# A recurrent attention kernel with a mixture of experts: a shorter lead-in, routing steps at other places of the order, and output scatters without an order among themselves

## The chip, the core and the metric

The kernel runs on one core of one Trainium2 chip. The metric is the device time of one execution in microseconds. Three runs of the kernel before gave 429.65, 430.54 and 431.69 us (median 430.54); the execution that the profiler recorded took 428.78 us, and its span from the first to the last instruction is 426.8 us. All times "at 133 us" below count from the start of that span.

Engines by the names of the profile: PE is the matrix engine (PEld its weight loads), DVE the vector engine, ACT the scalar engine, POOL the GpSimd engine and SP the sync engine, which here only issues DMAs. "SPq", "ACTq" and "POOLq" are the instruction queues of these engines.

## The reference

```python
# attention: B, H, S, D = 4, 8, 768, 48; everything is float32
for t in range(S):
    cur = einsum('bhd,bhe->bhde', u * k[t], v[t])
    y[t] = einsum('bhd,bhde->bhe', r[t], state + cur)
    state = w * state + einsum('bhd,bhe->bhde', k[t], v[t])
# bridge: x = y as N = 3072 rows of 384
# router and experts: E = 8, F = 1024
logits = normalised(x) @ normalised(expert_emb).T / tau
e = argmax(logits);  gate = softmax(logits)[e]
out[row] = gate[row] * (relu(x[row] @ w1[e]) @ w2[e])
```

Each row goes to one expert, and each expert's rows are computed together.

## The kernel before

**Attention.** The sequence is cut into 6 chunks of 128 steps; with 4 batches this makes 24 units (`i = 4 * chunk + batch`), and `attention` (L800 on) runs them one after the other, with the steps of several units interleaved in an order written out by hand (`tc.manual_schedule()`: the program order is the order on every engine). Within a unit, `turn_r` and `turn_k` transpose r and the scaled k on PE; the first is multiplied on DVE to `RT` (L328), the second copied by ACT to `KT` (L339). `scores` (L349) multiplies the two, `masked` (L355) writes the masked scores `AT` on DVE, and `sums` (L401, L410) multiplies them with V on PE, after which ACT copies the result to `yT` (L415). `rows` turns it back and adds, on DVE (L434), `xd`, the product of V with `diag`. That `diag` is reduced on DVE (`own_sum`, L303) from `KU`, two POOL products (`own`, L296 and L297) that need the tile `u_bc`, which ACT's queue loads (L123). In the order of DVE the reduction `diag` of a unit stands before the two `AT` of the same unit. Unit rows X go to a DRAM buffer `xs` (`put`, L618, SP's queue).

**Lead-in.** `build_first` (L46) loads the decay, makes its powers, turns them (`kpT`, L91) and scales the first k. It issues ten products of constants whose result is not used (`wake`, L67): six ahead of `kpT`, four behind it. `build_consts` then issues the other loads on ACT's queue, the constants on POOL, and copies on ACT.

**Router.** For each chunk (group) the steps `logits`, `choose`, `before`, `ranks`, `places`, `exps`, `gates`, `located`, `listed` and `taken` follow, spread over later units. `exps` (L601 to L604) is three small DVE operations and one exponential on ACT. `listed` calls `slices`, which makes two one-hot matrices on DVE (`lane` L637, `sel` L643) and from `sel` two POOL products (`what`, L647 and L648); `taken` (L663) multiplies `what` with `lane` on PE.

**Early experts.** After four of the six chunks `settle` (L699 to L721, ten DVE operations) names the two experts with the fewest rows so far (`LAST`), and SP loads their weights (w1 and w2, 1.5 MB each, both experts at once). One tile of rows of each is gathered (L931, POOL) and computed by `Early` while the router of the last chunks finishes; `fill(n)` puts n of its steps between steps of the router.

**Experts.** `experts` then works through eight blocks. Block i has up to four tiles of rows, gathered with indirect DMAs (L1001). Products use a seven-product scheme on halves: `weigh` and `weigh_out` combine the weights (`Sw`, `Tw`), `halves` combines the hidden rows (`Sh`), `hidden` and `out` do the products, `plain` does block 0's first layer in the usual way. Results are written to the output with indirect DMAs of POOL (`put`, L1259; `Early` at L966), each of which names the whole output tensor as its destination. [...]The last block ends with `out`, which puts two tiles.

Of the kernel before, what the change touches and what calls it, by code (L numbers as in the profile page):

```python
# [19 lines left out]
N = B * S  # L20
# [16 lines left out]
W_MIN, W_MAX = 0.7, 1.4  # L37
TS = 32
TG = TT // TM
WAKE = (6, 4)  # L40
AHEAD = 5


# [4 lines left out]
def build_first(k):  # L48


    nc, pool = k.nc, k.aconst
    wc = pool.tile([128, NP], F32, name="wc")
    nc.vector.memset(wc, 1.0)
    with nc.allow_non_contiguous_dma(reason="384 words"):
        for s, q in ((0, nc.sync), (1, nc.scalar)):
            q.dma_start(out=wc[s * DP : s * DP + D, :], in_=k.w.rearrange("(p s) d -> s d p", s=2)[s])
    k.ones = k.const.tile([128, 128], F32, name="ones")
    nc.vector.memset(k.ones, 1.0)
    wide = k.work.tile([128, 512], F32, name="wide", tag="AT1")
    nc.vector.memset(wide, 1.0)  # L60
    k.ident = k.const.tile([128, 128], F32, name="ident")
    make_identity(nc, k.ident)

    def wake(count):
        ps = k.ps.tile([128, 512], F32, name="wake", tag="y")
        for _ in range(count):
            nc.tensor.matmul(ps, k.ones, wide, start=True, stop=True)  # L67

    wake(WAKE[0])
    for lst, name, count in ((k.Kpad, "Kpad", 4), (k.Rpad, "Rpad", AHEAD + 2)):  # L70
        for i in range(count):
            t = pool.tile([128, H, DP], F32, name=f"{name}{i}")
            nc.gpsimd.memset(t[:, :, D:DP], 0.0)
            lst.append(t)
    load(k, 0, nc.scalar)


    nc.vector.tensor_scalar(wc, wc, W_MIN, W_MAX, ALU.max, ALU.min)
    t = pool.tile([128, NP, C], F32, name="wpow")
    for p in range(NP):  # L80
        nc.vector.tensor_tensor_scan(
            t[:, p, :], wc[:, p : p + 1].to_broadcast([128, C]), k.ones, 1.0, ALU.mult, ALU.mult
        )
    mid = pool.tile([128, NP], F32, name="mid")
    nc.vector.reciprocal(mid, t[:, :, C // 2])
    over_i = mid[:, :, None].to_broadcast([128, NP, C])
    kp = k.work.tile([128, NP, C], F32, name="kp", tag="AT0")
    nc.vector.tensor_mul(kp, t[:, :, ::-1], over_i)
    ps = k.ps.tile([128, NP, 2, DP], F32, name="kpT", tag="xp")
    for p in range(NP):  # L90
        nc.tensor.transpose(ps[:, p].rearrange("q s d -> q (s d)"), kp[:, p, :], k.ident)  # L91
    wake(WAKE[1])
    k.rpow = pool.tile([128, NP, C], F32, name="rpow")
    nc.vector.tensor_mul(k.rpow, t, over_i)
    cols = ps[:, :, :, 0:D]
    nc.vector.tensor_mul(
        k.Kpad[0].rearrange("q (p s) d -> q p s d", s=2)[:, :, :, 0:D],
        k.loaded[0][0].rearrange("q (p s) d -> q p s d", s=2), cols,
    )
    k.kpow = pool.tile([128, H, D], F32, name="kpow")  # L100
    nc.vector.tensor_copy(k.kpow.rearrange("q (p s) d -> q p s d", s=2), cols)  # L101
    k.wC = t[:, :, C - 1 : C].to_broadcast([128, NP, D])


# [8 lines left out]
def build_consts(k):  # L113
# [19 lines left out]
    k.wrow = k.aconst.tile([1, DM], F32, name="wrow")  # L133
    nc.scalar.dma_start(out=k.wrow, in_=k.w.rearrange("(o h) d -> o (h d)", o=1))
    k.yT = [k.aconst.tile([128, 2, NP // 2, C], F32, name=f"yT{i}") for i in range(2)]
    for t in k.yT:
        nc.gpsimd.memset(t, 0.0)
    for b in range(B):
        t = k.aconst.tile([128, NP, D], F32, name=f"state{b}")
        nc.gpsimd.memset(t, 0.0)  # L140
# [487 lines left out]
    return tile_, place  # L628


def slices(k, c, slots, tile_, place):


    nc, p = k.nc, k.rt
    n = slots.shape[1]
    lane = p.tile([128, B, 128], F32, name="lane", tag="lane", bufs=1)
    nc.vector.tensor_tensor(  # L637
        lane, k.lanes[:, None, :].to_broadcast([128, B, 128]),
        place[:, :, None].to_broadcast([128, B, 128]), ALU.is_equal,
    )  # L640
    sel = p.tile([128, B, n], F32, name="sel", tag="sel")
    full = [128, B, n]
    nc.vector.tensor_tensor(  # L643
        sel, slots[:, None, :].to_broadcast(full), tile_[:, :, None].to_broadcast(full), ALU.is_equal
    )
    what = p.tile([128, B, 2, n], F32, name="what", tag="what")
    nc.gpsimd.tensor_mul(what[:, :, 0, :], sel, k.token[:, c, :, None].to_broadcast(full))  # L647
    nc.gpsimd.tensor_mul(what[:, :, 1, :], sel, k.gate[:, c, :, None].to_broadcast(full))  # L648
    return lane, what


def located(k, g):
    g.spots = spots(k, g.c)


def listed(k, g):
    g.lane, g.what = slices(k, g.c, k.slots.rearrange("p e t -> p (e t)"), *g.spots)


def taken(k, g, tag="st"):  # L660
# [134 lines left out]
def attention(k):  # L795
# [17 lines left out]
    for i in range(-1, units):  # L813
        j = i - SETTLED * B
        if 0 < i + AHEAD < units:
            load(k, i + AHEAD)
        if i < 2:
            next(emb)
        whole(summed, i - 6)
        whole(places, i - 4)  # L820
        whole(logits_out, i - 3)
        on(turn_r, i + 1)
        if i < units - 1:
            on(own_rows, i, 0)
        on(turn_k, i + 1)
        whole(turn_logits, i - 3)
        on(scaled, i + 2)
        for n in (0, 1) if i < 0 else (i + 2,):
            on(own, n)
        on(states, i)  # L830
        of_group(squares, i - 1)
        if i < units - 1:
            on(own_rows, i, 1)
        whole(norms, i - 2)
        whole(choose, i - 3)
        whole(before, i - 3)
        whole(exps, i - 4)
        whole(located, i - 4)
        whole(gates, i - 5)
        whole(listed, i - 5)  # L840
        on(own_sum, i + 1)
        if i == units - 2:
            own_rows_once(k, i + 1)
        if j == 10:
            k.lists = turned_lists(k, perm, "st")
            lists = taken_by_rank(k, k.lists)
            first = [Early(k, r, *lists, w) for r, w in zip(LAST, k.weights)]
        on(sums, i)
        on(carry, i)
        on(scores, i + 1)  # L850
        on(masked, i + 1, 0)
        on(rows, i)
        on(masked, i + 1, 1)
        of_group(put, i)
        of_group(turn_rows, i - 1)
        whole(logits, i - 2)
        whole(ranks, i - 3)
        whole(taken, i - 5)
        if i == B:
            decays(k)  # L860
        if i == 2:
            build_turned(k)
        if 3 <= i < 3 + len(k.ring):
            k.nc.gpsimd.memset(k.ring[i - 3], 0.0)
        if j == 7:
            load_, count = loads(k, "st")
        if j == 8:
            settle(k, load_, count)
            for w, r in zip(k.weights, LAST):
                load_weights(k, expert_number(k, r), w)  # L870
        if j == 9:
            perm = turner(k, k.by)
        if j == 10:
            to = outs(k, lists[0], E * TM)

# [4 lines left out]
    def fill(count):  # L880
        for _ in range(count):
            next(early, None)

    gates(k, g)
    first[0].turn()
    turn_rows(k, h, B - 1)
    listed(k, g)
    squares(k, h, B - 1)
    norms(k, h)
    logits(k, h)  # L890
    first[1].turn()
    logits_out(k, h)
    fill(1)
    turn_logits(k, h)
# [6 lines left out]
    places(k, h)  # L901
    exps(k, h)
    located(k, h)
    summed(k, g)
    by = order(k, load_, k.settled)
    perm = turner(k, by)
    gates(k, h)
    listed(k, h)
    fill(4)
    taken(k, h, "tp")  # L910
    summed(k, h)
    fill(1)
# [9 lines left out]
class Early:  # L922
# [23 lines left out]
    def steps(self, to):  # L946
# [14 lines left out]
        for f in range(NF):  # L961
            nc.tensor.matmul(ps, self.hT[:, f, :], self.weights[1][:, f, :], start=(f == 0), stop=(f == NF - 1))
            if f == NF - 1:
                y = k.work.tile([128, DM], F32, name="earlyy", tag="xd")
                nc.scalar.mul(y, ps, self.gate)
                nc.gpsimd.indirect_dma_start(  # L966
                    out=k.out[:, :], out_offset=IndirectOffsetOnAxis(ap=to[:, self.col], axis=0), in_=y[:, :],
                    in_offset=None, bounds_check=N - 1, oob_is_err=False,
                )
            yield  # L970


# [23 lines left out]
def gather(k, take, to, gate, n=128):  # L996
# [6 lines left out]
        bounds_check=N - 1, oob_is_err=False,  # L1003
    )
    return G, to, gate, n


def gathers(k, r):
# [52 lines left out]
class Block:  # L1061
# [194 lines left out]

    def put(self, t, y):
        k, (_, j, _, here) = self.k, self.tiles[t]
        k.nc.gpsimd.indirect_dma_start(  # L1259
            out=k.out[:, :], out_offset=IndirectOffsetOnAxis(ap=k.to[0:here, j : j + 1], axis=0), in_=y[0:here, :],  # L1260
            in_offset=None, bounds_check=N - 1, oob_is_err=False,
        )


def combined(eng, t1, t2, t3, t4, b11, b12, b21, b22):
# [20 lines left out]
def experts(k):  # L1286
# [20 lines left out]
        b.turn()  # L1307
    do(blocks[1].Tx)
    do(blocks[1].weigh())
    blocks[0].plain()  # L1310
    first_weights(2)
    blocks[2].gather()
    do(blocks[0].halves())
    for i in range(E):
        doubled = blocks[i].weigh_out()
        for b in at(i + 1):
            b.hidden(doubled)
        do(doubled)
# [15 lines left out]
def all_lists(k):  # L1334

    nc = k.nc
    with ExitStack() as ctx:
# [1 line left out]
        slots = numbers(k, "allslots", [128, SLOTS], [[1, SLOTS]], 0, 0)  # L1339
        sums = k.ps.tile([128, 2, SLOTS], F32, name="allsums", tag="y")  # L1340
        for c in range(NCH):
            lane, what = slices(k, c, slots, *spots(k, c))
            for b in range(B):
                i = c * B + b
                nc.tensor.matmul(
# [91 lines left out]
def kernel(  # L1437
# [30 lines left out]
    n.x_dram = tc.dram_tile([128, S, D // 4], F32, name="x_dram")  # L1468
    n.need_dram = tc.dram_tile([E, TG], I32, name="need_dram")

    n.Rpad, n.Kpad, n.state = [], [], []
    for name in ("loaded", "KU", "diag", "xd", "RT", "KT", "at", "AT", "st", "y", "groups"):
        setattr(n, name, {})
    n.weights = [weight_tiles(n) for _ in range(2)]
# [43 lines left out]
```

## Time and profile before

| stretch, us | what runs | PE busy, us |
|---|---|---|
| 0 to 14 | lead-in | 14.0 (the unused products included) |
| 14 to 132 | units 0 to 21 | 116.5 of 118 |
| 132 to 144 | units 22, 23 | 10.2 of 12 |
| 144 to 160 | router of the last chunks, early experts begin | 11.5 of 16 |
| 160 to 178 | early experts | 17.3 of 18 |
| 178 to 412 | eight blocks | 232.4 of 234 |
| 412 to 427 | the last two scatters, end of the program | 0.3 of 15 |

The table is read from the busy time of each engine in each stretch. "Busy" counts an engine that is executing; where PE's figure falls short of the stretch, PE stood waiting. DVE is busy 251.1 us of the span, ACT 171.5, POOL 161.8.

### The profile page before, as it was taken

Reading aid. Unit: us, or ns where it says so; the run is one execution under the profiler, and the core shown is the slowest. Engines: PE = TensorE matmul, PEld = TensorE weight load, DVE = VectorE, ACT = ScalarE, POOL = GpSimd, SP = SyncE. Lnnn points to the kernel's source line nnn. Section 1 sums busy time; section 2 is a strip of 40 time slices with the busy share of each in tenths; the row PEclk is TensorE's granted clock in tenths of the full one; section 3 lists DMA queues with packets and bytes.
Section 4 is the critical chain, followed back from the end, with each engine's and each line's share of the span. In section 5 each row is a group of like instructions: output and inputs, shape, how many; then the busy total and the mean of one; then the engine's idle time right before and its main releaser. Section 6 shows DMA issues by size and latency. Waiting matters only on the chain. (4 is left out here: it accounts for less than half of the span.)

```text
span 426.8 us, 9300 instructions
## 1 busy us (share of the span) xinstructions
PE 399.8 (94%) x3556; PEld 355.6 (83%) x3556; DVE 251.1 (59%) x608; ACT 171.5 (40%) x517; POOL 161.8 (38%) x219
## 2 busy tenths in 40 slices
PE   8899999999999689999999999999999999999960
PEld 4688888888887578689999999999999999799660
DVE  4677786867688553137775767066376366566110
ACT  3487676767776301323323233223323323232110
POOL 7978777767673314210140241130330330300210
PEclk9999999999999999999999999999999999999995
DMA  9987676777715932133734424235255240320110
GB/s 165 189 181 154 137 150 127 149 151 150 151 39 183 389 133 88 35 75 131 251 126 149 166 77 154 81 138 185 58 179 172 62 172 28 112 92 17 39 42 21
DMA packets 93800, 54.39 MB, mean 127 GB/s; under 512 B 76937, under 2 KB 88380, under 8 KB 93746
## 3 DMA queue, kind: packets, MB, share of 16 engines
q1 hardware_dynamic: 89024, 43.85, 39.2%
q0 software_dynamic: 3296, 9.44, 6.8%
q8 instruction: 30, 0.49, 0.5%
q10 hardware_dynamic: 1426, 0.41, 0.4%
q14 instruction: 24, 0.20, 0.2%
HBM read 44.45 MB, written 9.63 MB: 127 GB/s over the span
## 5 line engine op out<-in xcount | busy, mean ns | idle before, releaser
L1259 POOL DMA_INDIRECT out_dram<-y,to x25 | 30.5, 1222 | 179.7 <-issue 91.5
L1135 PE MATMUL ps<-xTe,w 128*128 128x192 f32 (+3 forms) x336 | 63.0, 327 | 0.0
L1135 PEld LDWEIGHTS ps<-xTe,w 128*128 128x128 f32 x336 | 55.8, 190 | 0.5
L312 ACT ACTIVATE xd<-V,diag 128x48 f32<-128x48 f32 x184 | 46.3, 326 | 0.4 <-DVE diag L303 0.4
L355 DVE TENSOR_TENSOR AT<-at,umask 128x512 f32<-128x512 f32 x48 | 32.9, 686 | 23.1 <-PE at L349 23.1
L1142 ACT ACTIVATE hT<-hT 128x384 f32<-128x384 f32 (+3 forms) x42 | 22.0, 523 | 33.8 <-DVE hT L1165 21.1
L1199 PE MATMUL ps<-Tw,Sh 128*128 128x192 f32 x192 | 32.5, 326 | 0.0
L1199 PEld LDWEIGHTS ps<-Tw,Sh 128*128 128x128 f32 x192 | 31.4, 190 | 0.0
L349 PE MATMUL at<-RT,KT 48*128 48x128 f32 x384 | 27.9, 284 | 2.7 <-ACT yT L415 1.5
L1001 POOL DMA_INDIRECT G<-xs,take x25 | 26.3, 1053 | 9.8 <-PE ps L1135 2.7
L1135 PE MATMUL ps<-Tx,Sw 128*128 128x192 f32 (+3 forms) x168 | 29.7, 326 | 0.0
L349 PEld LDWEIGHTS at<-RT,KT 48*128 48x128 f32 x384 | 23.4, 187 | 7.3 <-issue 2.3
L1135 PEld LDWEIGHTS ps<-Tx,Sw 128*128 128x128 f32 x168 | 27.6, 190 | 0.1
L1152 DVE TENSOR_TENSOR u<-ps,p 128x384 f32<-128x384 f32 (+3 forms) x14 | 7.8, 557 | 31.7 <-PE ps L1135 30.9
L410 PE MATMUL y<-AT,V 128*48 128x128 f32 (+1 forms) x384 | 26.2, 277 | 0.0
L516 ACT COPY xT<-xp 128x384 f32<-128x384 f32 x24 | 11.5, 479 | 34.7 <-PE xp L514 34.7
L297 POOL TENSOR_TENSOR KU<-KU,Rpad 128x384 f32<-128x384 f32 x24 | 24.1, 1003 | 1.9
L296 POOL TENSOR_TENSOR KU<-K,u_bc 128x384 f32<-128x384 f32 x24 | 24.1, 1003 | 0.0
L288 POOL TENSOR_TENSOR Kpad<-K,kpow 128x384 f32<-128x384 f32 x23 | 23.0, 1000 | 1.7 <-DVE kpow L101 1.7
L1199 PE MATMUL ps<-w,hT 128*128 128x192 f32 x128 | 23.4, 326 | 0.0
L410 PEld LDWEIGHTS y<-AT,V 128*48 128x48 f32 (+1 forms) x384 | 20.2, 124 | 3.4 <-issue 3.4
L1199 PEld LDWEIGHTS ps<-w,hT 128*128 128x128 f32 x128 | 21.3, 190 | 0.3
(240 smaller groups left out, 810.7 us busy)
## 6 DMA issues: line engine op xcount, KB each, us to landing
w<-in_moe_w_dram SPq DMA_DIRECT2D x16, 1536.0 KB, 7.0
K<-in_k_dram SPq DMA_DIRECT2D x24, 192.0 KB, 3.2
V<-in_v_dram SPq DMA_DIRECT2D x24, 192.0 KB, 4.1
xs<-X SPq DMA_DIRECT2D x24, 192.0 KB, 2.0
Rpad<-in_r_dram SPq DMA_DIRECT2D x23, 192.0 KB, 4.0
G<-xs,take POOLq DMA_INDIRECT x27, 3.1
out_dram<-y,to POOLq DMA_INDIRECT x25, 3.1
Rpad<-in_r_dram ACTq DMA_DIRECT2D x1, 192.0 KB, 4.2
```

The costliest lines, as they stand in the source:

```text
L288: k.nc.gpsimd.tensor_mul(k.Kpad[i % len(k.Kpad)][:, :, 0:D], k.loaded[i][0], k.kpow)
L296: nc.gpsimd.tensor_mul(KU, K, k.u_bc)
L297: nc.gpsimd.tensor_mul(KU, KU, R[:, :, 0:D])
L312: k.nc.scalar.mul(k.xd[i][:, h, :], V[:, h, :], diag[:, h : h + 1])
L349: nc.tensor.matmul(at[s][:, p, :], KT[rows, p, :], RT[rows, p, :], start=True, stop=True)
L355: k.nc.vector.tensor_mul(a, k.at[i][s], k.umask[:, None, :].to_broadcast([128, NP, C]))
L410: mm(y[s][u * DP : u * DP + n, q, :], V[:, h * D : h * D + n], AT[s][:, p, :], start=(c == 0 and q == 0), stop=True, skip_group_check=True,)
L1001: nc.gpsimd.indirect_dma_start(out=G[0:n, :], out_offset=None, in_=k.xs[:, :], in_offset=IndirectOffsetOnAxis(ap=take[0:n], axis=0), bound ...
L1135: nc.tensor.matmul(ps[:, j, :], weights[:, (f + j) * 128 : (f + j + 1) * 128], moving, start=(first and j == 0), stop=True, skip_group_che ...
L1142: nc.scalar.activation(h, h, ACT.Relu)
L1199: nc.tensor.matmul(ps, a[:, f, :], b[:, f, :], start=(first and f == 0), stop=(f == NF // 2 - 1), skip_group_check=True)
L1259: k.nc.gpsimd.indirect_dma_start(out=k.out[:, :], out_offset=IndirectOffsetOnAxis(ap=k.to[0:here, j : j + 1], axis=0), in_=y[0:here, :], i ...
```

## The change

Six things are done.

1. Lead-in: three unused products instead of six before `kpT`, none behind it. `turn_r(k, 0)` and `turn_k(k, 0)` are called inside `build_first`, so that they and the copy to `KT` stand ahead of everything that `build_consts` issues. Two POOL memsets of `yT` are dropped. The preparation of the expert embedding (`build_experts`) is done in units 1 to 3 instead of -1 to 1.
2. `settle`, the first early expert's weight load and `turner` are done in unit 21, behind the reduction `diag`, instead of at the end of units 20 and 21. The second early expert's weights are loaded after the loop.
3. `exps` is done behind `sums` of its unit, not ahead of it.
4. `slices` is split: `lanes` makes the one-hot matrices, `chosen` makes `what`. For the last group `lanes` is done straight after `located`. The second `turn` of an early expert is done before `logits` of the last group, and `fill(6)` takes the place of `fill(4)`.
5. In `experts`, `weigh_out` of block 0 is done before `plain`, and `halves` of block 0 takes its place among the steps of block 1's `hidden`.
6. All output scatters go through `scatter`, which declares that they do not depend on one another.

```diff
-WAKE = (6, 4)
+WAKE = 3
-    wake(WAKE[0])
+    ps = k.ps.tile([128, 512], F32, name="wake", tag="tp")
+    for _ in range(WAKE):
+        nc.tensor.matmul(ps, k.ones, wide, start=True, stop=True)
...
-    wake(WAKE[1])
...
+    turn_r(k, 0)
     k.kpow = pool.tile([128, H, D], F32, name="kpow")
     nc.vector.tensor_copy(k.kpow.rearrange("q (p s) d -> q p s d", s=2), cols)
+    turn_k(k, 0)
...
-    for t in k.yT:
-        nc.gpsimd.memset(t, 0.0)
...
-        if i < 2:
+        if 1 <= i < 4:
             next(emb)
...
-        whole(exps, i - 4)
         whole(located, i - 4)
         whole(gates, i - 5)
+        whole(lanes, i - 5)
         whole(listed, i - 5)
         on(own_sum, i + 1)
+        if j == 9:
+            settle(k, load_, count)
+            load_weights(k, expert_number(k, LAST[0]), k.weights[0])
+            perm = turner(k, k.by)
...
         on(sums, i)
+        whole(exps, i - 4)
...
-        if j == 8:
-            settle(k, load_, count)
-            for w, r in zip(k.weights, LAST):
-                load_weights(k, expert_number(k, r), w)
-        if j == 9:
-            perm = turner(k, k.by)
...
+    load_weights(k, expert_number(k, LAST[1]), k.weights[1])
     gates(k, g)
     first[0].turn()
     turn_rows(k, h, B - 1)
+    squares(k, h, B - 1)
+    first[1].turn()
+    lanes(k, g)
     listed(k, g)
-    squares(k, h, B - 1)
     norms(k, h)
     logits(k, h)
-    first[1].turn()
...
     located(k, h)
+    lanes(k, h)
     summed(k, g)
...
-    fill(4)
+    fill(6)
...
+def scatter(k, y, to):
+    put = k.nc.gpsimd.indirect_dma_start(
+        out=k.out[:, :], out_offset=IndirectOffsetOnAxis(ap=to, axis=0), in_=y, in_offset=None,
+        bounds_check=N - 1, oob_is_err=False,
+    )
+    for earlier in k.scattered:
+        k.tc.declare_no_dep(put.ins, earlier, reason="each token's row is in one tile")
+    k.scattered.append(put.ins)
...
     do(blocks[1].weigh())
+    do(blocks[0].weigh_out())
     blocks[0].plain()
...
-    do(blocks[0].halves())
     for i in range(E):
-        doubled = blocks[i].weigh_out()
+        doubled = blocks[i].weigh_out() if i > 0 else blocks[0].halves()
```

More of the change, by code (lines that the diff above doesn't have):

```diff
@@ L62, in build_first @@
     make_identity(nc, k.ident)
[L64 to L67, printed above, removed]
-    wake(WAKE[0])
+    ps = k.ps.tile([128, 512], F32, name="wake", tag="tp")
+    for _ in range(WAKE):
+        nc.tensor.matmul(ps, k.ones, wide, start=True, stop=True)
     for lst, name, count in ((k.Kpad, "Kpad", 4), (k.Rpad, "Rpad", AHEAD + 2)):
@@ L628, in spots, with slices @@
     return tile_, place
-def slices(k, c, slots, tile_, place):
+def slices(k, slots, tile_, place):
     nc, p = k.nc, k.rt
@@ L645, in slices, with chosen, lanes @@
     )
-    what = p.tile([128, B, 2, n], F32, name="what", tag="what")
+    return lane, sel
+def chosen(k, c, sel):
+    nc = k.nc
+    n = sel.shape[2]
+    full = [128, B, n]
+    what = k.rt.tile([128, B, 2, n], F32, name="what", tag="what")
     nc.gpsimd.tensor_mul(what[:, :, 0, :], sel, k.token[:, c, :, None].to_broadcast(full))
     nc.gpsimd.tensor_mul(what[:, :, 1, :], sel, k.gate[:, c, :, None].to_broadcast(full))
-    return lane, what
+    return what
 def located(k, g):
     g.spots = spots(k, g.c)
+def lanes(k, g):
+    g.lane, g.sel = slices(k, k.slots.rearrange("p e t -> p (e t)"), *g.spots)
 def listed(k, g):
-    g.lane, g.what = slices(k, g.c, k.slots.rearrange("p e t -> p (e t)"), *g.spots)
+    g.what = chosen(k, g.c, g.sel)
 def taken(k, g, tag="st"):
@@ L821, in attention @@
         whole(logits_out, i - 3)
-        on(turn_r, i + 1)
+        if i >= 0:
+            on(turn_r, i + 1)
         if i < units - 1:
             on(own_rows, i, 0)
-        on(turn_k, i + 1)
+        if i >= 0:
+            on(turn_k, i + 1)
         whole(turn_logits, i - 3)
@@ L965, in steps @@
                 nc.scalar.mul(y, ps, self.gate)
[L966 to L969, printed above, removed]
+                scatter(k, y, to[:, self.col])
             yield
@@ L1258, in put @@
         k, (_, j, _, here) = self.k, self.tiles[t]
[L1259 to L1262, printed above, removed]
+        scatter(k, y[0:here], k.to[0:here, j : j + 1])
 def combined(eng, t1, t2, t3, t4, b11, b12, b21, b22):
@@ L1341, in all_lists @@
         for c in range(NCH):
-            lane, what = slices(k, c, slots, *spots(k, c))
+            lane, sel = slices(k, slots, *spots(k, c))
+            what = chosen(k, c, sel)
             for b in range(B):
@@ L1469 @@
     n.need_dram = tc.dram_tile([E, TG], I32, name="need_dram")
-    n.Rpad, n.Kpad, n.state = [], [], []
+    n.Rpad, n.Kpad, n.state, n.scattered = [], [], [], []
     for name in ("loaded", "KU", "diag", "xd", "RT", "KT", "at", "AT", "st", "y", "groups"):
```

## The prediction

> **What bounds the kernel now.** I read four views in this order: the page, who waited for whom on PE, busy time and clock by stretch, and the timeline at both ends. First, the page and PE's waits:
>
> ```profile
> span 426.8 us, 9300 instructions
> ...
> PE 399.8 (94%) x3556; PEld 355.6 (83%) x3556; DVE 251.1 (59%) x608; ACT 171.5 (40%) x517; POOL 161.8 (38%) x219
> ```
> ```profile
> PE early_x L942 <- DMA G<-xs,take: 2.2, 1, 2.2
> PE take L663 <- POOL what L648: 2.0, 1, 2.0
> ...
> PE at L349 <- ACT yT L415: 1.5, 2, 1.0
> PE ps L1135 <- DVE p L1155: 1.1, 1, 1.1
> PE yrows L428 <- ACT yT L415: 1.0, 1, 1.0
> ```
>
> PE is the bound, and its named waits are few and each is short (columns: total us, times, longest). So the kernel gains only what those waits cost, plus what the two ends hold, where PE's busy time is not useful work or is none. The next view, busy time in one-microsecond stretches (PE, PEld, DVE, ACT, POOL, then granted clock, DMA share, GB/s), shows a loss that counts as busy:
>
> ```profile
> 148.00:149.00 1.00, 0.85 (x16) 0.76 (x17) 0.65 (x2) 0.61 (x3) 0.27 (x1) 0.51 1.05 369
> 149.00:150.00 1.00, 1.00 (x10) 0.61 (x4) 0.00 (x0) 0.27 (x1) 1.00 (x3) 0.50 1.07 373
> 150.00:151.00 1.00, 1.00 (x7) 1.00 (x6) 0.50 (x1) 0.00 (x0) 0.48 (x1) 0.50 1.11 380
> 151.00:152.00 1.00, 1.00 (x11) 0.83 (x12) 0.25 (x2) 0.00 (x0) 0.00 (x0) 0.79 1.03 367
> ```
>
> After the idle stretch of 142.5 to 146.7, PE ran at half clock for 3.4 us, a loss of 1.7 us. Last, the timeline of both ends (start, duration, idle before):
>
> ```profile
> 1.62 6.91 PE L67 MATMUL wake<-wide,ones 128*128 128x512 f32 x12 [1.62 <-DVE wide L60]
> 8.37 0.60 PE L91 MATMUL kpT<-ident,kp 128*128 128x128 f32 x4
> 8.80 3.60 PE L67 MATMUL wake<-wide,ones 128*128 128x512 f32 x8
> ...
> 13.95 1.16 PE L349 MATMUL at<-RT,KT 48*128 48x128 f32 x16 [0.68 <-ACT KT L339]
> ```
> ```profile
> 412.26 0.97 POOL L1259 DMA_INDIRECT out_dram<-y,to  x1 [6.34 <-DVE y L1222]
> 412.37 0.42 DVE L1226 SCALAR_TENSOR_TENSOR y<-ps,gates,v 128x192 f32<-128x192 f32 x1 [0.88 <-PE ps L1199]
> 416.56 0.98 POOL L1259 DMA_INDIRECT out_dram<-y,to  x1 [3.32 <-DVEq L1369]
> ```
>
> `kpT` stands behind unused products although DVE finished its input at 5.80. The last scatter's rows are ready at 412.79, but it starts at 416.56, a landing time after the one before it. I don't believe the releaser named there (a branch); in the program that scatter waits for the previous one.
>
> **What the Trainium skill says.** "TensorE: Matmul & The Clock Gate", Part 1: the array runs at half rate after about one idle window of 3.4 us and returns after one busy window. The trace agrees (0.50 for 3.4 us). "DMA: Bandwidth & Descriptors", Queues, rings and completion order: each DMA engine takes turns between queue rows, a whole packet at a time. The trace agrees in kind: the early gathers took 6.4 and 6.1 us to land beside the weight loads at 370 GB/s, against a median of 3.1. Same page, Anatomy of one DMA: some 2 us of a DMA are fixed, mostly the write receipt. The shortest scatter here lands in 1.9 us.
>
> **The lead-in.** The 12 records of the first six products took 6.91 us; the later eight took 3.60, 0.45 each. The first six records therefore took 6.91 - 6 x 0.45 = 4.2 and three products end at 5.8. Then `kpT` 0.60, scaling on DVE 0.56, `kt` 0.60, copy `KT` 0.59: first scores at about 8.3 instead of 13.95. That looks like 5.6 us. It isn't: `turn_k` now puts ACT's copy of `KT`, which waits for PE, ahead of ACT's issue of the `u_bc` load, which moves from 1.86 to about 8.2. `KU` needs `u_bc`, `diag` needs `KU`, and on DVE both `AT` stand behind `diag`. Landing takes between 2.3 us (the decay load, 0.90 to 3.17) and 4.6 (`u_bc` itself, then behind another load on its queue); I take 3.2, so 11.4. `KU` 2.1, `diag` 0.55, two `AT` 1.3, `RT` of unit 1 0.65 give the second scores at 11.4 + 4.7 = 16.1, against 18.05: a gain of 1.95. Behind `u_bc` on ACT stand three small loads that each wait for an earlier transfer, the eight casts (1.4 us) and the first `xd`; they are through by 12.8, before `diag` is, so they cost nothing. PE is out of work from about 11.3 (scores 0, `rt`, `kt`, `st` of 1.16, 0.6, 0.6, 0.6) to 14.7: 3.4 us idle, which I expect to cost half clock, 1.7 at most; some of it lies beside waits, I take 1.4. The embedding's four DVE operations (0.9) leave unit 1, where they caused the 0.43 us wait included above, and go ahead of `RT` in unit 3, which had 1.07 to spare; two small ones join unit 4's `RT`, which already holds PE up 0.59: 0.35. The dropped memsets (0.99) were hidden on POOL. Net 1.95 - 1.4 - 0.35 = 0.2; bounds -2.0 (`u_bc` at 12.8, full loss of clock) and +2.0.
>
> **The middle.** `settle` is ten DVE operations from 129.43 to 131.88; they held up `RT` and so PE 1.04 us at 131.8. Behind `diag` that wait goes. But DVE's work is not less: `AT`, X and `AT` of unit 22 then begin at 134.1, and by unit 23 PE is only about 0.8 ahead. `exps` behind `sums` lets the first `yT` copy go before the exponential, which waited for DVE till 142.9: `yrows` from 143.47 to 142.1. Its three DVE operations (0.55) lie in slack. The early gather depends on DVE's list and starts 0.36 earlier (139.86). Only the first expert's weights now run beside it, issued about 134.4 instead of 132.4 because `settle` ends later: 3.1 MB at 0.39 MB/us, until about 144.4. I put the gather at 145.4 instead of 146.7 (bounds 144.5 and 146.3). SP puts units 21 to 23 before the second weights. From there: half clock again but partly over idle time, the second early transpose in front of `logits`, then `lg` at 149.6 instead of 151.5. The router chain from `cp` to the last `what` keeps its length except that `lane` and `sel` (0.66 + 0.28) go before the gate: `taken` at about 157.2 instead of 159.26, and `fill(6)` covers the 2.0 us wait, leaving 0.2. PE work from there to the end of the early experts falls from 17.4 to 16.0, two steps having gone ahead: end at 173.2 against 176.7. Gain 3.5; bounds 1.0 and 5.5. The second weights are issued at about 144.5 and needed at 161; two loads together take some 10, so nothing waits.
>
> **The blocks.** DVE's four `Sh` (189.76 to 192.3) held up PE 1.12 at 193.1. `Tw` of block 0 (4 x 0.95) now lies under `plain` (10.5 us, DVE idle 6.8 before it), `Sh` among block 1's steps. Gain 1.1. Unordered scatters shift gathers earlier, but PE waits for no gather there: nothing.
>
> **The end.** The last scatter can start 0.3 after the one before is issued: 413.5 instead of 416.56, 3.0. Everything after it on POOL (flag, branch, end) follows; bounds 2.5 and 3.1.
>
> Sum: 0.2 + 3.5 + 1.1 + 3.0 = 7.8 us of the profiled span of 426.8. That execution took 428.78, the median is 430.54; I take the difference from the median: 422.7.
>
> **Rivals.** (A) As above, 422.7: 0.53. (B) The clock stays up in both idle stretches and the gather lands at 144.5: 1.4 + 1.2 + 0.8 more, 419.3. For it: the windows run free of the program. Against: a stretch 45% busy (144.6 to 148) cost the clock. 0.22. (C) The waits only move: `u_bc` takes its 4.6 us (lead-in -1.5), the gather still takes 6.4 and PE stands in order behind the second one (middle 1.0); 430.54 + 1.5 - 1.0 - 1.1 - 3.0 = 426.9. Speaks for it that four queues are full at both places. 0.16. (D) Slower: the second expert's weights come too late. They are issued 12 us after where they were; the early expert needs them at 161, and each microsecond beyond that is lost. To pass the gain they must take over 161 - 144.5 + 7.8 = 24 us; the slowest weight load here took 15.3. At 27, 433. 0.04. (E) The scatters keep an order, by a shared semaphore: end 0, 425.7. In the built program each waits for the transfer eight indirect DMAs earlier, long landed. 0.05.
>
> **How the numbers follow.** A measurement here can tell about 0.5% (2.15 us) from no change. B and A hold 0.75, C down to 426.9 is half taken in: range 419.0 to 426.5. Faster: A, B, most of C and E, 0.89; same, the rest of C and E, 0.07; slower 0.04.
>
> **What would show it.** Right: `u_bc`'s KU at 11 to 12, second scores near 16, clock near 0.5 around 15 to 18, no PE wait at 132 or on `what`, the last scatter 1.3 after the one before. Wrong: first `AT` before 12 (then `diag` does not bind), a PE wait on a weight load at the second early expert, or an end that stays 10 us behind PE's last product because another engine sets it.

## The result, and the profile after

| | before | after |
|---|---|---|
| median of four runs, us | 430.97 (429.65 to 431.69) | 425.33 (424.43 to 425.64) |
| ratio, 95% interval | | 0.9869 (0.9839 to 0.9899) |
| profiled execution: time, span, us | 428.78, 426.8 | 425.64, 423.8 |

The kernel became 5.6 us faster; 7.8 was forecast. The forecast of 422.7 was too low, its range of 419.0 to 426.5 held the time. The two profiled executions lie only 3.0 apart: that of before was faster than all four runs in the table (428.78 against 429.65 to 431.69), that of after the slowest of its four. So the medians say how much each part is worth, and the traces say where it happens. With four runs a side, a difference between two medians below is good to about 1.3 us (0.3%). The experiments were timed in four other sessions, with a median of before of 430.49 to 431.12 beside them.

The page of after, the lines that stand against those of before:

```profile
span 423.8 us, 9269 instructions
...
PE 398.1 (94%) x3542; PEld 355.1 (84%) x3542; DVE 251.6 (59%) x608; ACT 171.4 (40%) x517; POOL 160.0 (38%) x217
```

And PE's waits (who waited for whom; total us, times, longest):

```profile
PE y L406 <- DVE AT L351: 4.4, 1, 4.4
PE early_x L955 <- DMA G<-xs,take: 2.8, 1, 2.8
...
PE yrows L424 <- ACT yT L411: 0.9, 1, 0.9
...
PE ps L225 <- ACT xT L512: 0.6, 1, 0.6
PE take L672 <- POOL what L653: 0.5, 1, 0.5
```

Three waits of before are gone or small: the one at settle (1.04), the one on `p` in block 1 (1.1), the one on `what` (2.0, now 0.5). The wait for the early gather is still there (2.2, now 2.8), and so is the one for `yT` (1.0, now 0.9). One is new and the longest of all: 4.4 us in the lead-in. The timeline of after tells how it came about (start, duration, engine and line, then in brackets the idle time before and its releaser):

```profile
1.62 5.44 PE L66 MATMUL wake<-wide,ones 128*128 128x512 f32 x6 [1.62 <-DVE wide L60]
6.90 0.60 PE L88 MATMUL kpT<-ident,kp 128*128 128x128 f32 x4
...
8.84 0.58 ACT L335 COPY KT<-kt 128x512 f32<-128x512 f32 x1 [5.70 <-PE kt L333]
8.84 0.35 ACTq L121 DMA_DIRECT2D u_bc<-in_u_dram  x1
...
9.47 1.16 PE L345 MATMUL at<-RT,KT 48*128 48x128 f32 x16 [0.67 <-ACT KT L335]
...
13.35 0.99 POOL L292 TENSOR_TENSOR KU<-K,u_bc 128x384 f32<-128x384 f32 x1 [3.11 <-DMA K<-in_k_dram]
...
15.44 0.55 DVE L299 TENSOR_REDUCE diag<-KU 128x8 f32<-128x384 f32 x1 [6.28 <-POOL KU L293]
15.91 1.28 DVE L351 TENSOR_TENSOR AT<-at,umask 128x512 f32<-128x512 f32 x2
...
16.64 1.71 PE L406 MATMUL y<-AT,V 128*64 128x128 f32 x16 [4.39 <-DVE AT L351]
18.29 2.08 PE L345 MATMUL at<-RT,KT 48*128 48x128 f32 x16
...
149.51 0.55 PE L955 MATMUL early_x<-ident,G 128*128 128x128 f32 x3 [2.79 <-DMA G<-xs,take]
...
411.95 0.98 POOL L1020 DMA_INDIRECT out_dram<-y,to  x1 [7.11 <-issue]
412.06 0.42 DVE L1247 SCALAR_TENSOR_TENSOR y<-ps,gates,v 128x192 f32<-128x192 f32 x1 [0.88 <-PE ps L1220]
413.24 0.98 POOL L1020 DMA_INDIRECT out_dram<-y,to  x1 [0.30 <-issue]
```

The same steps in the timeline of before:

```profile
1.86 0.72 ACTq L123 DMA_DIRECT2D u_bc<-in_u_dram  x1
...
11.06 0.99 POOL L296 TENSOR_TENSOR KU<-K,u_bc 128x384 f32<-128x384 f32 x1
...
13.48 0.54 DVE L303 TENSOR_REDUCE diag<-KU 128x8 f32<-128x384 f32 x1
...
15.14 1.29 DVE L355 TENSOR_TENSOR AT<-at,umask 128x512 f32<-128x512 f32 x2 [1.11 <-PE at L349]
...
18.05 1.16 PE L349 MATMUL at<-RT,KT 48*128 48x128 f32 x16 [0.43 <-ACT yT L415]
```

The first scores come at 9.47 instead of 13.95. The load of `u_bc` is issued at 8.84 instead of 1.86, because it now stands behind the copy to `KT` that waits for PE. `KU` follows at 13.35, `diag` at 15.44, `AT` at 15.91, and PE stands from 12.26 to 16.64. The second scores come at 18.29; before it was 18.05. All of the head start is lost here. (The releaser that the trace puts beside `KU`, a load of K, is not the cause; the first experiment decides that, and the trace of the run with the middle undone, whose lead-in is the same, names the `u_bc` load itself.) The last scatter starts 1.29 us after the one before it; it was 4.30. The span still ends 11.8 us behind PE's last product (14.5 before), 10.6 behind the start of the last scatter (10.2 before): the end moved with that scatter.

The busy time and clock by stretch of after show a second loss (columns: stretch, sum, PE, PEld, DVE, ACT, POOL with counts, then granted clock, DMA share, GB/s):

```profile
14.00:15.00 1.00, 0.00 (x0) 0.00 (x0) 0.00 (x0) 0.00 (x0) 0.92 (x2) 1.00 1.09 219
...
16.00:17.00 1.00, 0.36 (x6) 0.36 (x8) 1.00 (x2) 0.97 (x5) 0.92 (x2) 1.00 1.00 191
17.00:18.00 1.00, 1.00 (x14) 0.77 (x10) 1.00 (x3) 1.00 (x5) 1.00 (x2) 0.56 1.04 201
...
23.00:24.00 1.00, 1.00 (x19) 0.87 (x19) 0.63 (x2) 0.70 (x2) 0.92 (x2) 0.53 0.74 190
24.00:25.00 1.00, 1.00 (x22) 0.83 (x18) 0.35 (x1) 1.00 (x6) 0.83 (x2) 1.00 1.08 216
```

The clock falls just after PE has gone back to work and stays at half until 24: in stretches of 0.1 us it falls in 17.1 to 17.2 and is back in 23.9 to 24.0, 6.8 us later. Third scores, before and after:

```profile
22.59 1.16 PE L349 MATMUL at<-RT,KT 48*128 48x128 f32 x16
```
```profile
24.97 1.16 PE L345 MATMUL at<-RT,KT 48*128 48x128 f32 x16
```

From unit 4 on, after lies 3.2 us behind before, and it makes that up only in the middle, the blocks and the end.

### The profile page after: what moved, and what is told of

It is laid out like the page before. It is cut to its first block, busy times and chain, and to the rows that moved or that the text cites. A ratio compares the mean times of both kernels' runs of the same rounds, so it can differ in the third digit from the quotient of the medians.

```text
span 423.8 us, 9269 instructions
## 1 busy us (share of the span) xinstructions
PE 398.1 (94%) x3542; PEld 355.1 (84%) x3542; DVE 251.6 (59%) x608; ACT 171.4 (40%) x517; POOL 160.0 (38%) x217
## 4 chain that ended last, share of the span: by engine, by line
PE 80%; POOL 6%; DMA 5%; issue 3%; DVE 2%; SPq 2%; ACT 0%; POOLq 0%; ACTq 0%
PE ps L1156 24%; PE ps L1220 15%; PE ps L1260 5%; PE at L345 4%; PE y L406 4%; PE ps L1273 4%; PE ps L1134 2%; PE ps L1104 2%; PE early_y L975 2%; PE y L397 2%; PE kt L333 2%; PE early_h L966 2%; PE st L366 2%; PE yrows L424 2%; PE rt L322 2%
## 5 line engine op out<-in xcount | busy, mean ns | idle before, releaser
L345 PE MATMUL at<-RT,KT 48*128 48x128 f32 x384 | 28.8, 291 | 1.3 <-ACT KT L335 0.7
```

The lines of the kernel that those rows point to most:

```text
L345: nc.tensor.matmul(at[s][:, p, :], KT[rows, p, :], RT[rows, p, :], start=True, stop=True)
```

## The experiments

The theory: each part of the change is worth about what the prediction says, but for the lead-in, which loses 3.2 us (the lag at the scores of unit 4 and after) because one queue (ACT's) holds the `u_bc` load behind a waiting copy. The rivals: it is the missing unused products that cost the clock; or the gather that lost the time. Every kernel is the changed one with the edit shown, unless said otherwise.

**The `u_bc` load alone, moved back ahead.**

```diff
     load(k, 0, nc.scalar)
+    k.u_bc = k.aconst.tile([128, H, D], F32, name="u_bc")
+    nc.scalar.dma_start(out=k.u_bc..., in_=...u...)    # and taken out of build_consts
```

> The changed kernel with one move: ACT issues the u_bc load straight behind the load of r for unit 0, ahead of the wait for kt and the KT copy. Theory (the queue of ACT starves KU): the first KU product starts right behind the second Kpad product, at about 10.2 us instead of 13.35; diag(0) at 12.3, AT at 12.8, PE's idle time behind st of unit 0 shrinks from 4.39 to about 1.3 us, the stretch at half clock disappears, second scores at about 15.2 instead of 18.29 and third scores at about 20 instead of 24.97. Time about 420.5 (425.3 - 4.8). Rival (taking the unused products out leaves the clock to fall anyway): PE keeps a stretch at 0.5 between 14 and 24 us, third scores not before 22.5, time 422.5 to 424. Rival (the load of u_bc isn't what KU waits for): KU still starts at about 13.3, time 425.3.

Measured: 420.94 us (420.03 to 422.13), 4.4 less than the changed kernel. Its timeline:

```profile
1.86 0.72 ACTq L74 DMA_DIRECT2D u_bc<-in_u_dram  x1
...
10.22 1.00 POOL L292 TENSOR_TENSOR KU<-K,u_bc 128x384 f32<-128x384 f32 x1
...
13.53 1.25 PE L406 MATMUL y<-AT,V 128*64 128x128 f32 x16 [1.25 <-DVE AT L351]
```

`KU` starts the moment POOL is through with `Kpad`, PE's idle time is 1.25 instead of 4.39, the clock stays at 1.00 in every microsecond from 10 to 26. Second scores come at 14.82, third at 19.37. One DMA issue decides the lead-in; the unused products as such weren't needed to hold the clock. Of the 5.6 us gained at the third scores 4.7 are left from unit 4 on: units 3 and 4 then wait 0.7 each for ACT's `xd` and for `RT`.

**The whole lead-in undone, and the lead-in alone.** The first has ten unused products, `turn_r` and `turn_k` of unit 0 in the loop, the memsets and the embedding as before. The second is the kernel before with the new lead-in only.

```diff
-WAKE = 3
+WAKE = (6, 4)
...
-    turn_r(k, 0)
-    turn_k(k, 0)
...
-        if 1 <= i < 4:
+        if i < 2:
             next(emb)
```

> The changed kernel with the lead-in of the kernel before: ten unused products, turn_r and turn_k of unit 0 back in the loop, yT memsets, embedding in units -1 to 1. Theory: the lead-in of the changed kernel lost 3.2 us at the scores of unit 21, so the time falls to about 422.1. Rival (as the prediction had it, the lead-in is worth +0.2, and what it loses is made up by waits later): 425.3 to 425.5.

> The kernel before with the new lead-in and nothing else. Theory: slower by about 3.2 us, 434.2, with the same idle time of some 4.4 us and the same stretch at half clock. Rival (the idle time at settle at 132 and at the gather at 143 takes up what is late by then, since what PE waits for there doesn't depend on PE): 431 to 432.

Measured: 423.37 (423.09 to 423.64), 2.0 less; and 432.66 (431.80 to 433.41) against 430.79 of before in the same session, ratio 1.0053 (1.0033 to 1.0072), 1.9 more. Both ways the lead-in costs 2 us, not the 3.2 that I read off the pair of traces; both expectations missed by over 1 us. The trace of the first explains the gap. The twelve records of the six unused products at the start (the trace has two for each product),

```profile
1.62 8.16 PE L67 MATMUL wake<-wide,ones 128*128 128x512 f32 x12 [1.62 <-DVE wide L60]
```

take 8.16 us here and took 6.91 in the profiled execution of before. The moment at which PE goes from 0.9 to 0.45 us a record differs by execution. So the trace of before started 1.25 us luckier than this one, and that stood in the 3.2: against the trace of this run the changed kernel is only 1.95 late at the scores of unit 21 (129.79 against 127.84). The second run's figure lies between its theory and its rival, that the waits at 132 and 143 take up the delay. Its trace speaks against the rival: it is 3.4 us behind before at the scores of unit 21 (129.93 against 126.56) and 3.5 at the first product of block 0 (180.91 against 177.42).

**The wait filled with unused products.** What PE waits for stays.

```diff
+        if i == 0:
+            ps = k.ps.tile([128, 512], F32, name="warm", tag="xp")
+            for _ in range(4):
+                nc.tensor.matmul(ps, k.ones, k.rpow..., start=True, stop=True)
         on(sums, i)
```

> The changed kernel with four unused products (8 records of 0.45 us) put on PE behind st of unit 0, in the middle of the wait for AT that lasted from 12.26 to 16.64. What PE waits for is not touched, so this takes away the loss of clock alone. Theory (the idle time costs twice, once as a wait and once by the stretch at half clock behind it): second scores at about 17.9 instead of 18.29, the third at about 22.6 instead of 24.97, no 0.50 in the clock before 24; time about 423 (425.3 - 2.4), about what undoing the whole lead-in gave (423.4). Rival (the clock falls whatever PE does at this place): third scores at 24.5 or later, time 425 or more.

Measured: 424.21 (423.17 to 424.81), 1.1 less. The clock holds at 1.00:

```profile
12.00:13.00 1.00, 1.00 (x4) 0.52 (x3) 0.00 (x0) 0.44 (x5) 0.70 (x1) 1.00 1.17 235
...
17.00:18.00 1.00, 1.00 (x17) 0.88 (x17) 0.47 (x2) 1.00 (x5) 1.00 (x2) 1.00 1.24 206
```

From first to third scores it takes 12.72 us against 15.50, so the clock alone is 2.8 us in this pair of traces. Of these 0.8 are given back in units 3 and 4, where DVE and ACT can't follow (waits of 0.72, 0.57 and 0.70 against 0.57 and 0.59): an `AT` of DVE takes 0.69 us at half clock (20.40 in after) and at full clock (19.21 in before). The medians show 1.1 of the expected 2.4, with an error of about the same size. So the idle time does cost twice, but how much of the 2 us is clock stays uncertain. A likely reason, not tested by itself, is in the other traces with this lead-in. In that of the middle undone (below) the clock was back after 3.4 us (15.7 to 19.1):

```profile
15.00:16.00 1.00, 0.58 (x8) 0.47 (x8) 1.00 (x3) 1.00 (x5) 0.92 (x2) 0.85 1.31 217
...
19.00:20.00 1.00, 1.00 (x10) 0.80 (x8) 0.82 (x2) 0.12 (x1) 1.00 (x3) 0.94 1.28 177
```

The run without weights beside the gathers had 3.4 us too; after, the lead-in alone, scatters in order and block 0 undone had 6.8, and late weights (the first of the three gather runs) 10.2, part of it while PE still stood. So the loss of clock differs by execution.

**`u_bc` ahead, and `KU` of unit 0 ahead of `Kpad` on POOL.**

```diff
     nc.gpsimd.memset(k.fresh[:, :, 0:1], 0.0)
+    own(k, 0)
...
-        for n in (0, 1) if i < 0 else (i + 2,):
+        for n in (1,) if i < 0 else (i + 2,):
```

> The changed kernel with the u_bc load ahead of the KT copy on ACT (as in the run before that did this alone, 420.94) and, in addition, the two KU products of unit 0 at the end of the constants on POOL, ahead of the second Kpad product, in POOL's idle time from 6.3 to 9.2. Theory: KU from about 6.5 to 8.5, diag(0) no later than 9.2, AT limited by scores(0) at 10.6, so PE's remaining idle time of 1.25 us goes: second scores at 13.6 instead of 14.82, time about 419.7. Rival (PE's next limit takes over at once, kt of unit 1 or the landing of R): second scores unchanged, 420.9.

Measured: 419.34 (418.74 to 420.03); against before 0.9739 (0.9699 to 0.9780). This version beats both kernels, the changed one by 6.0 us. In its timeline `KU` starts as soon as `u_bc` has landed, 5.2 us after its issue at 1.86, and `AT` waits for the scores and no longer for `diag`:

```profile
7.07 1.00 POOL L293 TENSOR_TENSOR KU<-K,u_bc 128x384 f32<-128x384 f32 x1 [0.72 <-DMA u_bc<-in_u_dram]
...
10.29 1.29 DVE L352 TENSOR_TENSOR AT<-at,umask 128x512 f32<-128x512 f32 x2 [0.56 <-PE at L346]
```

**The middle undone, block 0 undone, the scatters in order again.** Three parts, each put back as it was in the kernel before.

```diff
# middle
+        if j == 8:
+            settle(k, load_, count)
+            for w, r in zip(k.weights, LAST):
+                load_weights(k, expert_number(k, r), w)
...
# block 0
-    do(blocks[0].weigh_out())
     blocks[0].plain()
...
+    do(blocks[0].halves())
# scatters
-    for earlier in k.scattered:
-        k.tc.declare_no_dep(put.ins, earlier, reason=...)
```

> The changed kernel with the middle of the kernel before: settle, both weight loads and turner at their old places, exps ahead of sums, one-hot matrices with what, the old order of the early turns, four steps filled. Theory from the two traces: settle's wait of 1.04 and the waits behind the gather come back, 2.4 us, so about 427.7. As the prediction had it: 3.5 us, 428.8. Rival (waits only move): 1.0 us, 426.3.

> The changed kernel with block 0's weigh_out behind plain and its halves ahead of the loop, as before. By the prediction and by both traces the wait of 1.12 us on DVE's p at block 1's hidden products comes back and nothing else changes: 426.4. Rival (the wait is made up for later in the blocks, or the gathers move): within 0.4 us of 425.3.

> The changed kernel without the declaration that the scatters don't depend on one another. Theory: only the end changes, the last scatter starts a landing time after the one before it, so 3.0 us more: 428.3. Rival (the order of the scatters also held back gathers in the blocks, or the end of the program waits for all landings anyway): more than 4 or less than 1 us.

Measured: middle undone 428.65 (20 runs, 426.76 to 430.37), 3.3 more; block 0 undone 426.71 (426.64 to 426.85), 1.4 more; scatters in order 428.10 (10 runs, 426.95 to 430.38), 2.8 more. For the middle, the two traces say less: with it undone the trace is 1.8 us ahead at the logits of the second chunk (68.77 against 70.59, the start again) and 0.6 behind at the first product of block 0, so 2.4. First the changed kernel, then the middle undone:

```profile
178.25 1.53 PE L1104 MATMUL ps<-ident,G 128*128 128x128 f32 x12 [0.73 <-ACT earlyy L978]
```
```profile
178.82 1.53 PE L1105 MATMUL ps<-ident,G 128*128 128x128 f32 x12 [0.73 <-ACT earlyy L979]
```

The kernel before and the run with the lead-in undone give 2.8: from the scores of unit 21 to block 0, 50.86 us (126.56 to 177.42) against 48.02 (127.84 to 175.86). For block 0, the 1.4 is about as large as its error, but the line of before is back among PE's waits:

```profile
PE ps L1156 <- DVE p L1176: 1.1, 1, 1.1
```

For the scatters, the end of the timeline has its gap again:

```profile
412.38 0.97 POOL L1020 DMA_INDIRECT out_dram<-y,to  x1 [7.11 <-DVE y L1241]
412.49 0.42 DVE L1245 SCALAR_TENSOR_TENSOR y<-ps,gates,v 128x192 f32<-128x192 f32 x1 [0.88 <-PE ps L1218]
417.33 0.97 POOL L1020 DMA_INDIRECT out_dram<-y,to  x1 [3.98 <-DVEq L1386]
```

The rows are ready at 412.91, the scatter starts 4.4 us later. Nothing differs between the two kernels but the declaration, so it is the order, and not the branch that is named as releaser.

**The early gather and the weights beside it.** In the changed kernel the first early gather is issued at 142.59 and its rows are used at 149.51, 6.9 us later, though now only one expert's weights run beside it. The first edit moves these weights behind both gathers; the second does that on top of the best version; the third also puts the second early turn behind `logits` again.

```diff
-            load_weights(k, expert_number(k, LAST[0]), k.weights[0])     # behind settle
...
             to = outs(k, lists[0], E * TM)
+            load_weights(k, expert_number(k, LAST[0]), k.weights[0])
...
# third run only
-    first[1].turn()
     lanes(k, g)
...
     logits_out(k, h)
-    fill(1)
     turn_logits(k, h)
+    first[1].turn()
+    fill(1)
```

> The changed kernel with the first early expert's weights loaded behind both early gathers in the order of the program (after the put of X of unit 22 instead of behind settle), some 6 us later. Theory (the early gather is slow because it shares the DMA engines with that load): the first gather, issued at 142.6, lands about 3.1 us after its issue is through or by about 146, PE's wait of 2.79 for it goes, logits of the last group come 2.5 to 3 us earlier, the weights still arrive before they are needed at about 150; time about 422.5. Rival (a gather takes 6 to 7 us at this place whatever else runs): wait and time unchanged, 425.3. Other rival (the weights then come too late): a PE wait on them at the first steps of the early expert, 426 or more.

> All three moves on the changed kernel: u_bc load ahead, KU of unit 0 ahead, the first early weights behind the early gathers. If the lead-in and the middle are separate places the gains add: 425.3 - 4.4 - 1.2 - 2.8, about 416.9. If the gather isn't helped, about 419.7.

> The run with all three moves (421.33), and in it the second early turn put back behind logits of the last group, and the first early step behind turn_logits. Theory (there PE waited 2.9 us for the second gather, which fell into the weights just as the first had, because the change's order puts its turn ahead of logits): the wait goes or falls behind lg, lg at about 143.5 instead of 147.76, a short wait for the second gather or for w1 of at most 1.5 us, time about 418.5, a little under the 419.34 without the late weights. Rival (the early weights are now the bound, PE waits for them in full): 421 or more.

Measured: 427.00 (426.63 to 428.73), 1.7 more than the changed kernel; 421.33 (419.94 to 421.81), 2.0 more than the best version; 421.77 (421.03 to 422.44), 2.4 more. In none of the three did the gain come that the theory expected. The first gave the figure of its other rival (the weights come too late), but PE waits for no weight load in its trace; the second gave neither of its figures; the third gave its rival's. The timeline of the first shows why:

```profile
145.09 0.07 SPq L250 DMA_DIRECT2D w<-in_moe_w_dram  x1
...
147.06 0.49 PE L955 MATMUL early_x<-ident,G 128*128 128x128 f32 x3
...
151.52 0.90 PE L955 MATMUL early_x<-ident,G 128*128 128x128 f32 x3 [3.18 <-DMA G<-xs,take]
```

The first gather's rows are there without a wait. The second gather is issued 1.6 us later and falls into the weights that now follow; it needs 7 us, and its turn stands ahead of `logits`. The wait changed its gather, and a stretch at half clock from 151.1 to 157.9 came with it. With the second turn behind `logits` (third run) PE reaches `lg` at 143.19, 4.6 us earlier than in the second run, and gains nothing:

```profile
144.71 0.55 PE L956 MATMUL early_x<-ident,G 128*128 128x128 f32 x3 [1.19 <-DMA G<-xs,take]
146.83 0.99 PE L967 MATMUL early_h<-earlyx,w 128*128 128x128 f32 x6 [1.58 <-DMA w<-in_moe_w_dram]
```

PE waits for that gather, then for the weights; and on DVE the copy of the second early rows stands ahead of the operations that read `lg`, so the router waits too (first of them at 145.77).

**No weights beside the gathers at all.** The kernel loads the weights of experts 0 and 1 in unit 8, ahead of `settle`; what it leaves out is the choice of the two experts, so the early rows meet other experts' weights.

```diff
-            load_weights(k, expert_number(k, LAST[0]), k.weights[0])
...
+        if j == -4:
+            for n in (0, 1):
+                load_weights(k, n, k.weights[n])
...
-    load_weights(k, expert_number(k, LAST[1]), k.weights[1])
```

> The changed kernel with the weights of both early experts loaded in unit 8, for two experts fixed in advance and not for the ones that settle names, so the rows of the early experts get other experts' weights and their values are not the reference's; everything else is computed as before. No weight load then lies beside the early gathers. Theory (6.4 to 6.9 us of an early gather are the sharing with the weight load): both gathers land 3 to 3.5 us after they are issued at about 142.6 and 144.2, PE's wait of 2.79 for the first is gone or under 0.5, and no stretch at half clock follows; logits of the last group come some 3 us and the end of the early experts 3 to 3.5 us earlier, time about 422. Rival (gathers at this place take 6 us by themselves, or PE waits as long for something else, such as the second yT): time above 424.5.

Measured: 425.66 (425.21 to 427.34), no gain. The rival's figure, but not for its reason. What the trace says of the gathers' tile `G`, first here, then in the kernel before:

```profile
DMA to landing us min/median/max: 3.1/3.3/3.4
```
```profile
DMA to landing us min/median/max: 6.1/6.3/6.4
```

So the sharing with the weights about doubles the landing. From the scores of unit 23 to the first product of block 0 this kernel takes 33.84 us (144.88 to 178.72) and the changed one 37.66 (140.59 to 178.25): 3.8 are gained there. They are lost before: the 6 MB in unit 8 stand in SP's queue ahead of loads of k and r. POOL's `Kpad` waits 6.1 us for its k, PE waits once for 3.50 us (`take` at 89.39), and the clock is at half from 87.6 to 94.5, so unit 23 comes 4.3 late.

## Why the prediction was right and where it was wrong

The four terms of the sum, against the runs that put one part back (changes of the median):

| part | forecast, us | measured, us |
|---|---|---|
| lead-in | +0.2 (bounds -2.0, +2.0) | -2.0 |
| middle | 3.5 (1.0, 5.5) | 3.3 (2.4 and 2.8 by traces) |
| blocks | 1.1 | 1.4 |
| end | 3.0 (2.5, 3.1) | 2.8 |
| sum | 7.8 | 5.5; the change itself 5.6 |

That the parts add up so closely is in part luck. Taken as ratios to the kernel before of the same session, they are -1.7, 3.8, 1.4 and 3.2, in sum 6.7; each has an error of about 1.5.

**The lead-in failed**; it came out at the lower bound that was given for it. Its mechanism was named rightly: the `u_bc` load behind the copy, `KU`, `diag`, `AT`, an idle PE, then half clock. Four sizes were wrong, all to the same side, and the term, put at +0.2, measured -2.0.

- "Three products end at 5.8": they end at 7.06. I had taken the moment of full clock from one execution of before. "TensorE: Matmul & The Clock Gate", Part 1, of the Trainium skill says that the window runs free of the program and that the moment of transition varies with it. The runs agree: the six records of the three products took 4.69 to 5.49 us, and 5.44 in the profiled execution of after.
- Landing of `u_bc` "I take 3.2": `KU` starts 4.5 after the issue (4.0 with the middle undone). The figure of before for this very load, 4.6, was one end of my bracket and the nearer one.
- Idle PE 3.4 us: 4.39.
- Half clock "1.7 at most", one window: it lasted from 17.1 to 24.0, 6.8 us; from second to third scores PE took 6.68 us instead of 4.54, so 2.1 were lost there. The same part of the skill reckons with a busy window of about 3.4 us until the clock returns, and its table says one or more; here it took 6.8, two such lengths, though PE was busy without a break from 17 on. With the middle undone one length was enough. Why it is one or two stays open.

Second scores "near 16" were 18.29. The embedding cost 0.57 (PE waits in unit 3 for ACT's `xT`, since its transposes share a buffer with those of X) and not 0.35.

The reading that a stretch "45% busy (144.6 to 148)" cost the clock was off: the trace of before has PE busy for 1.22 of these 3.40 us, 36%.

**The middle** came out in size by the medians, 3.3; the traces give 2.4 and 2.8. Settle's wait is gone: the scores of unit 21 come 3.23 us later than before, those of unit 22 2.11 later, so 1.1 are gained. I had doubted that PE would keep it, and it does. `what` holds PE up for 0.54 instead of 2.02. The part behind `taken` went as worked out: 16.1 us to the end of the early experts (161.40 to 177.52), forecast 16.0. The step on the gather was too hopeful and gained nothing: less the 3.2 us of delay its rows come at 146.3, my upper bound, not 145.4. "Only the first expert's weights now run beside it" is true and doesn't help: with one expert's weights beside it the gather needed 6.9 us, with two 6.4, with none 3.3, for beside one load the DMA engines already move 350 to 420 GB/s (142 to 148 in after). "DMA: Bandwidth & Descriptors", Queues, rings and completion order, has each DMA engine take turns between queue rows; these numbers agree in kind, as one saturating queue is enough. The wait for `yT` was to go as well and stayed, 0.9; it cost nothing, as PE then stands until the gather's rows are there. Why the medians give the middle 0.5 to 0.9 more than the traces is open; it lies within the error.

**The blocks and the end** went as worked out. The wait at block 1 left and came back with its edit, and the last scatter starts 1.29 us after the one before it.

**The rivals.** A gave the direction and three of the terms. By the number alone, E (425.7) and C (426.9) lie nearer to 425.3 than A (422.7); that is luck for E, whose mechanism did not occur. C was right on one of its two places, "lead-in -1.5", and on a gather that is no faster; its middle of 1.0 was too small. B is out, the clock fell in both idle stretches. D didn't occur: PE runs from 166.83 through the second early expert without a wait. E is out by the scatters' own run.

## What to carry to other kernels

When a step is pulled ahead on an engine that also issues DMAs, list the DMA issues that now stand behind its wait and follow each to its first reader: here one load, issued 7 us later, ate a head start of 4.5 us, and putting it back was worth 4.4. Filler on the matrix engine is only worth taking out if real work is ready to follow, because an idle stretch of some 4 us was paid a second time here, by stretches of 3.4 to 10.2 us at half clock. And a transfer that saturates the DMA engines isn't taken out of a gather's way by moving it behind that gather if a second gather follows.

## What the runs showed that I had not expected

- A stretch at half clock ahead of PE's last product lasted 3.4, 6.8 or 10.2 us in every trace here, whole multiples of 3.4: after an idle time of 4.4 us 6.8 (17.1 to 24.0), of 3.9 us with the middle undone 3.4 (15.7 to 19.1), in the run with late weights 6.8 (151.1 to 157.9). Two executions of one kernel can thus differ by such a stretch, which costs up to 1.7 us (an estimate: half of 3.4).
- At the start of an execution the granted clock is shown as 1.00 while the products run at half their rate (0.9 against 0.45 us a record); the change comes at a different time in each execution, and shifted what follows by 1.25 us between the two traces with twelve such records.
- A gather of 128 rows took 6.4 us to land beside two experts' weights, 6.9 beside one's, 3.3 beside none.
